# A linear-attention block and a gated FFN on one core: queues in a new written order, one PSUM ring, 64-row products together, matmuls on zeros

## The chip, the cores and the metric

The kernel runs on one core of a Trainium2 chip. A core has four engines with instruction queues of their own that work in order: TensorE (PE in the profile; its weight loads are the row PEld), VectorE (DVE), ScalarE (ACT) and GpSimd (POOL). SyncE (SP) only issues DMAs; GpSimd issues DMAs too, and its queue (q0) can cast float32 to float16 on the way. The metric is the device time of one execution in microseconds (us), lower is better.

## What is computed

```python
# q, k, v: (8 batches, 8 heads, 576 positions, 64)
q_s = softmax(q, axis=-1)                     # over the 64 features
k_s = softmax(k, axis=2)                      # over the 576 positions
kv  = einsum('bhsd,bhse->bhde', k_s, v)       # a 64x64 matrix for each head
x   = einsum('bhsd,bhde->bhse', q_s, kv)      # -> (4608 tokens, 512)
a, b = x @ w1, x @ w2                         # (4608, 1024) each
out = ((a * b) @ w3) @ w_out                  # (4608, 512)
```

All inputs and the output are float32; the matrix products run in float16 with float32 accumulation.

## The kernel before

**Folding.** `w3 @ w_out` is worked out once, in eight row blocks `ft`: `w3t` (line 441) transposes a block of w3 on TensorE, `w3T` copies it out of PSUM, `pf` (line 451, eight matmuls of 512 columns a block) multiplies it with w_out, and `W3O` scales it out of PSUM. `pf.ft.0` needs the first half of w_out (`wo.0`), `pf.ft.1` the second.

**Attention, for each batch b.** On k: `kmx` (maximum over positions), `cb` (the same across partitions, a chain of small VectorE steps), `ksub`, `kexp`. On q, in two parts p (four and five of nine position groups; 1024 and 1280 elements a partition): `qmx`, `qsub`, `qexp`, `qsm` (sum), `qeps`, `qrc` (reciprocal), `qn`. The normalized q is transposed on TensorE for batches 0 and 1 (`qt`, line 642, then the copy `qT`) and by a DMA on SP for the others (`qd`). `kv` (lines 562 and 571) multiplies k and v, `kv2` divides, and the product with q comes in three pieces: `xm.b.0` and `xm.b.1` (four matmuls of 64 rows and 512 columns each, line 668) and the rest `xt.b` (eight of 64 columns, the same line). `xs` and `xts` scale them out of PSUM into x. v is cast by the load in batches 0 and 1 and by `vc` in the others.

**FFN, for each chunk c** (one for each batch, and a ninth of the positions that `xt` left over). For each of eight blocks u, `up.1` (x @ w2, line 793), its copy `bs` out of PSUM, `up.0` (x @ w1, the same line), and `ab` (line 808), the product of both on VectorE; each `up` is four matmuls of 128 rows and 512 columns. Chunk 1 is worked in two halves. Then four `down` (line 815; 830 in the ninth chunk), eight matmuls each, whose results `os` copies out of PSUM and `st` stores from SP.

**PSUM.** It has eight banks. Before, they are three pools: four banks for `pab` (up, w3t), two for `po` (down, pf) and two for `att` (kv, qt, xm, xt). A product `xm` or `xt` takes two banks, so the next one waits until `xs` has emptied both.

**The order.** `Plan` holds the steps with their needs. `Plan.order` walks through time with a length in us for each step, `LEADS` (an offset for each kind of step) and `PICKS` (which engine takes a step that has a choice), and emits the steps in the order that it finds; `LOADS` gives the order of the first loads. Within 50 us of that walk, `link` makes a step of VectorE or GpSimd that uses their shared port wait for the last one of the other engine. Loads of q, k and v of batch 0 and 1 and of the weights go out on GpSimd (only `q.0.0` on SP), those of later batches on SP in the order k, q, v. SP's first load of batch 2 waits until `w1.2`, the last load on GpSimd but one, has landed. On GpSimd a load waits until the eighth before it has landed.

Of the kernel before, what the change touches and what calls it, by code (L numbers as in the profile page):

```python
# [13 lines left out]
ALU = mybir.AluOpType  # L14
# [3 lines left out]
class Plan:  # L18


    RATE = 409.0e3
    LAND = 1.7
    HOP = 0.15
    NEAR = 0.2
    LINKED = 50.0
    BUS = 2.2
    BEGIN = {"SP": 0.74, "POOL": 1.25, "DVE": 1.0, "ACT": 1.0, "PE": 1.0}

    def __init__(self, rings, leads, picks):
        self.rings = rings  # L30
        self.leads = leads
        self.picks = picks
        self.steps = {}

    @staticmethod
    def key(name):


        if name[0] == "up":
            return f"up{name[1]}_{min(name[2], 3)}"  # L40
        if len(name) > 2 and name[1] < 2 and name[0] not in ("bs", "ab", "down", "os", "st", "pf"):
# [892 lines left out]
```

## Time and profile before

| | |
|---|---|
| three runs | 245.95, 247.72 and 247.88 us (median 247.72) |
| the profiled execution | 244.56 us, of which the span from first to last instruction is 242.7 us |
| TensorE busy | 227.2 us (94%), 1884 matmuls |
| VectorE busy | 180.3 us (74%) |
| ScalarE, GpSimd busy | 120.4 us (50%), 118.2 us (49%) |
| first matmul, end of the last | 9.9 us, 239.4 us |
| read from memory, written | 38.80 MB, 9.44 MB |

Busy time is counted per engine, so overlapping work counts on each. TensorE's matmuls are pipelined, and a busy TensorE is not one at its peak. The chain of waits follows back from the last instruction what released it, and so names the work that set the end; an engine off that chain costs nothing by being idle.

### The profile page before, as it was taken

How to read it: one execution, taken by the hardware profiler on the slowest of the kernel's cores; microseconds unless marked ns; L12 is line 12 of the kernel's file. 1: busy time of each engine (PE TensorE's matmuls, PEld its weight loads, DVE VectorE, ACT ScalarE, POOL GpSimd, SP SyncE). 2: the span in 40 equal slices, each digit the busy share in tenths (PEclk: the TensorE clock that was granted, in tenths of full speed). 3: DMA queues.
4: the chain of work that ended last, by engine and by line, in shares of the span. 5: the costliest groups of instructions: out<-in, count | busy, mean ns of one | idle time of the engine just before them, and what ended most of it. 6: DMA issues, size and time to landing. Idle time of an engine off the chain costs nothing.

```text
span 242.7 us, 4757 instructions
## 1 busy us (share of the span) xinstructions
PE 227.2 (94%) x1884; PEld 112.1 (46%) x1884; DVE 180.3 (74%) x306; ACT 120.4 (50%) x183; POOL 118.2 (49%) x79
## 2 busy tenths in 40 slices
PE   0398899999999999999999999999999999999994
PEld 0245644454886444344444444444444344444443
DVE  2889869969998989989998999799876154335320
ACT  2367767536867657545543664466433522121112
POOL 8446276508996788279445946595462000000000
PEclk9999999999999999999999999999999999999999
DMA  6999999999998994993999089801940230022153
GB/s 229 234 265 251 260 298 196 248 398 391 354 151 292 388 171 123 399 219 67 324 384 177 0 309 375 173 4 36 131 108 3 58 72 0 3 64 66 43 130 130
DMA packets 37766, 45.65 MB, mean 188 GB/s; under 512 B 15985, under 2 KB 21873, under 8 KB 37745
## 3 DMA queue, kind: packets, MB, share of 16 engines
q1 hardware_dynamic: 30080, 34.74, 50.9%
q0 software_dynamic: 7664, 10.62, 20.4%
q8 instruction: 14, 0.23, 0.4%
q14 instruction: 8, 0.06, 0.1%
HBM read 38.80 MB, written 9.44 MB: 199 GB/s over the span
## 4 chain that ended last, share of the span: by engine, by line
PE 90%; DMA 6%; POOL 2%; issue 1%; ACT 1%; ACTq 0%; POOLq 0%
PE pab L793 52%; PE po L815 23%; DMA w<-in_moe_w_dram 6%; PE po L451 4%; PE po L830 3%; PE pkv L562 2%; PE xm L668 2%; PE w3t L441 1%; PE xt L668 1%; PE qtp L642 1%; POOL w L403 1%; PE pkv L571 1%; ACT w3T L342 0%; POOL wosb L403 0%; POOL k L403 0%
## 5 line engine op out<-in xcount | busy, mean ns | idle before, releaser
L808 DVE TENSOR_TENSOR ab<-pab,bsb 128x512 f16<-128x512 f32 x72 | 49.0, 687 | 24.8 <-PE pab L793 19.3
L793 PE MATMUL pab<-x,w2sb 128*128 128x512 f16 (+1 forms) x288 | 65.9, 356 | 0.0
L793 PE MATMUL pab<-x,w1sb 128*128 128x512 f16 (+1 forms) x288 | 65.9, 356 | 0.0
L815 PE MATMUL po<-W3O,ab 128*128 128x512 f16 x256 | 59.3, 380 | 0.0
L342 ACT CAST bsb<-pab 128x512 f16<-128x512 f32 x49 | 28.5, 582 | 40.6 <-PE pab L793 40.5
L793 PEld LDWEIGHTS <-w1sb 128*128 128x128 f16 x320 | 30.7, 98 | 30.0
L793 PEld LDWEIGHTS <-w2sb 128*128 128x128 f16 x320 | 30.5, 98 | 29.3 <-issue 0.2
L537 POOL TENSOR_TENSOR k<-k,cb 128x1152 f32<-128x1152 f32 x14 | 36.5, 2623 | 10.5 <-issue 7.9
L627 POOL TENSOR_TENSOR en<-eq,qr 128x1024 f16<-128x1024 f16 (+1 forms) x14 | 29.3, 2096 | 21.9 <-issue 9.1
L815 PEld LDWEIGHTS <-ab 128*128 128x128 f16 x256 | 23.8, 98 | 29.7 <-issue 2.9
L595 POOL TENSOR_TENSOR q<-q,qm 128x1280 f32<-128x1280 f32 (+1 forms) x13 | 27.7, 2145 | 13.7 <-DVE rc L580 11.7
L342 ACT COPY osb<-po 128x512 f32<-128x512 f32 (+1 forms) x28 | 15.9, 569 | 35.8 <-PE po L815 31.0
L479 DVE TENSOR_REDUCE km<-k 128x128 f32<-128x1152 f32 x12 | 25.8, 2149 | 0.0
L590 DVE TENSOR_REDUCE qm<-q 128x16 f32<-128x1024 f32 (+1 forms) x16 | 21.5, 1345 | 5.7 <-DMA q<-in_q_dram 5.7
L603 ACT ACTIVATE eq<-q 128x1024 f16<-128x1024 f32 (+1 forms) x16 | 18.6, 1164 | 13.7 <-POOL q L595 6.9
L545 ACT ACTIVATE ek<-k 128x1152 f16<-128x1152 f32 x16 | 18.6, 1163 | 6.5 <-POOL k L537 5.1
L608 DVE TENSOR_REDUCE qr<-eq 128x16 f32<-128x1024 f16 (+1 forms) x16 | 21.2, 1324 | 0.1
L342 DVE CAST bsb<-pab 128x512 f16<-128x512 f32 x23 | 15.8, 685 | 5.2 <-PE pab L793 4.0
L451 PE MATMUL po<-wosb,w3T 128*128 128x512 f16 x64 | 16.8, 408 | 1.2 <-issue 0.6
L346 ACT ACTIVATE x<-xm 128x512 f16<-128x512 f32 x30 | 16.5, 598 | 1.7 <-PE xm L668 1.7
L441 PE MATMUL w3t<-ident,w 128*128 128x128 f16 x64 | 5.8, 249 | 11.0 <-DMA w<-in_moe_w_dram 11.0
L342 ACT COPY w3T<-w3t 128x1024 f16<-128x1024 f16 x8 | 8.0, 1016 | 6.4 <-PE w3t L441 5.9
(60 smaller groups left out, 172.0 us busy)
## 6 DMA issues: line engine op xcount, KB each, us to landing
out_dram<-osb SPq DMA_DIRECT2D x66, 128.0 KB, 2.4
k<-in_k_dram SPq DMA_DIRECT2D x6, 1152.0 KB, 5.8
q<-in_q_dram SPq DMA_DIRECT2D x6, 1152.0 KB, 9.3
v<-in_v_dram SPq DMA_DIRECT2D x6, 1152.0 KB, 11.9
k<-in_k_dram POOLq DMA_DIRECT2D x2, 1152.0 KB, 10.8
q<-in_q_dram POOLq DMA_DIRECT2D x2, 640.0 KB, 14.7
v<-in_v_dram POOLq DMA_DIRECT2D x2, 576.0 KB, 12.9
w<-in_moe_w_dram POOLq DMA_DIRECT2D x2, 512.0 KB, 10.9
```

The costliest lines, as they stand in the source:

```text
L342: return [(nc.scalar.copy if eng == "ACT" else engine[eng].tensor_copy)(out=out, in_=in_)]
L451: nc.tensor.matmul(st["pf", ft], lhsT=st["w3T", ft][:, gt, :], rhs=wosb[:, gt, :], start=(gt == 0), stop=(gt == N_FT - 1))
L479: dve.tensor_reduce(out=st["km", b][:, two(hp), :], in_=kb[:, two(hp), :, :].rearrange("p h j d -> p h d j"), axis=AX.X, op=ALU.max)
L537: return [engine[eng].tensor_tensor(out=kb[:, two(hp), :, :], in0=kb[:, two(hp), :, :], in1=st["cb", b][:, two(hp), None, :].broadcast_to( ...
L545: nc.scalar.activation(out=st["ek", b][:, hp, :, :].rearrange("p j (i d) -> p i j d", i=2), in_=kb[:, two(hp), :, :], func=AF.Exp)
L590: dve.tensor_reduce(out=st["qm", b][:, :, j], in_=qb[:, :, j, :], axis=AX.X, op=ALU.max)
L595: return [engine[eng].tensor_tensor(out=qb[:, :, j, :], in0=qb[:, :, j, :], in1=st["qm", b][:, :, j, None].broadcast_to([P, HH, n, D]), op ...
L608: dve.tensor_reduce(out=st["qr", b][:, :, slice(*PARTS[p])], in_=st["eq", b, p], axis=AX.X, op=ALU.add)
L627: return [engine[eng].tensor_tensor(out=st["en", b][:, j, :, :].rearrange("p j h d -> p h j d"), in0=st["eq", b, p], in1=st["qr", b][:, :, ...
L793: nc.tensor.matmul(st["p", one, c, sub, u][:, a * (t1 - t0):(a + 1) * (t1 - t0)], lhsT=w[:, ct, fb * P:(fb + 1) * P], rhs=x()[:, ct, t0:t1 ...
L808: dve.tensor_tensor(out=st["ab", c][:, nf * u:nf * u + nf, t0:t1], in0=cut(st["p", 0, c, sub, u]), in1=cut(st["bsb", c, sub, u]), op=ALU.mult)
L815: nc.tensor.matmul(st["po", c, tb], lhsT=st["ab", c][:, ft, tb * P:(tb + 1) * P], rhs=W3O[:, ft, :], start=(ft == 0), stop=(ft == N_FT - 1))
```

## The change

- **The order is written out.** `Plan.order`, `LEADS`, `PICKS` and `LOADS` are gone. `ORDER` names each step once, with `/A`, `/D` or `/P` for ScalarE, VectorE or GpSimd where there is a choice, and `Plan.run` emits them in that order; each engine's queue is the part of it that the engine has. `late` and `kind` only describe steps. `link` is made along the whole order, up to the last step of VectorE that uses the port.
- **Loads.** On GpSimd the order is q.0.1, k.0, w3.4, w3.2, wo.0, wo.1, w3.1, q.1.1, w3.0, v.0, w3.3, k.1, w2.0, w1.0, w2.1, w1.1, q.1.0, w2.2, w1.2, w2.3, w1.3, v.1, w3.5. Before it was k.0, w3.4, wo.0, w3.2, wo.1, q.0.1, w3.0, q.1.0, w3.3, v.0, w3.5, q.1.1, w3.1, w2.0, k.1, w1.0, w2.3, w2.1, w1.1, w2.2, w1.3, w1.2, v.1. So w3.5 (blocks 6 and 7 of the fold) moves from the eleventh place to the last, and these two blocks are folded at the start of chunk 1. SP's first load of batch 2 is now q.2, and waits (`GATE = 3`) until w1.3, the third from the end, has landed; q.2, q.3, v.2, k.2 follow in this order.
- **Engines.** VectorE gets four `w3T`, one `W3O`, `ksub.1.0`, `ksub.1.1`, `qsub.1.1`, `qn.1.0` and four more `xs` than before, and gives up `qsub.0.1` (now on GpSimd), both `qT` and three `xts`; in the later batches some `bs`, `os` and `qn` change places too.
- **PSUM** is one ring of eight banks for everything: a new tile takes the bank of the tile eight before it and waits until that is free.
- **The 64-row products** xm.b.0, xm.b.1 and xt.b stand next to each other in TensorE's queue in all batches but batch 1, where xm.1.0 and xm.1.1 are neighbours and xt.1 follows kv.2. Before, four to eight `pf`, `up` or `down` matmuls or more stood between them.
- **43 matmuls on zeros** of 512 columns: 13 and 20 ahead of the first transposes of w3, 10 between the third of these and `pf.2.0`. VectorE sets the zeros beforehand.
- The second identity matrix, which nothing used, is gone.

```diff
+    def text(name):
+        return ".".join(str(x) for x in name)
+
+    def run(self, order, link):
+        byname = {self.text(n): s for n, s in self.steps.items()}
+        listed = [t.partition("/")[::2] for t in order.split()]
+        assert sorted(t for t, _ in listed) == sorted(byname), set(byname) ^ {t for t, _ in listed}
+        twos = [i for i, (t, c) in enumerate(listed) if byname[t]["port"] and self.CODES.get(c, "DVE") == "DVE"]
         held = None
+        for i, (t, code) in enumerate(listed):
+            s = byname[t]
+            eng = s["eng"]
+            if isinstance(eng, tuple):
+                eng = self.CODES[code]
+                assert eng in s["eng"], t
+                got = s["emit"](eng)
+            else:
+                got = s["emit"]()
+            if s["port"] and eng != "ACT" and held and i <= twos[-1] and held[0] != eng:
+                link(got[0], held[1])
+            if s["port"] and eng != "ACT":
+                held = eng, got[-1]
+
+
+EARLY = [("q", 0, 0)]
+GATE = 3
...
+ORDER = """
+zero.0 q.0.0 qmx.0.0 qsub.0.0/D zero.1 q.0.1 qmx.0.1 qexp.0.0 qsm.0.0 k.0 kmx.0.0 cb.0 w3.4 ident w3t.5 w3.2
+w3t.2 w3t.4 zero.2 w3T.5/D wo.0 w3T.2/A pf.2.0 pf.5.0 wo.1 pf.5.1 pf.2.1 w3.1 q.1.1 w3.0 v.0 w3.3 qsub.0.1/P
+qexp.0.1 qeps.0.0/D ksub.0.1/D kexp.0.1 w3T.4/A k.1 qrc.0.0 qn.0.0/P qt.0.0 qT.0.0/A w2.0 w3t.1 pf.4.0 pf.4.1
+qsm.0.1 qeps.0.1/D qrc.0.1 ksub.0.0/D w1.0 qn.0.1/P w3T.1/D W3O.2/A W3O.4/A kexp.0.0 W3O.5/A qmx.1.1
+qsub.1.1/D qexp.1.1 w3t.0 w3T.0/D pf.1.0 qt.0.8 qT.0.8/A pf.1.1 W3O.1/D kv.0 qt.0.16 qsm.1.1 qeps.1.1/A w3t.3
+qT.0.16/A w3T.3/A pf.0.0 pf.0.1 W3O.0/A qrc.1.1 kv2.0 xm.0.0 xs.0.0.0/A xm.0.1 xs.0.1.0/A xt.0 xts.0.1/A
+xs.0.0.1/A xs.0.1.1/A pf.3.0 qn.1.1/D pf.3.1 W3O.3/A kmx.1.0 cb.1 qt.1.8 qT.1.8/A xts.0.0/A qt.1.16 up.1.0.0.0
+bs.0.0.0/A up.0.0.0.0 up.1.0.0.1 up.0.0.0.1 bs.0.0.1/A ksub.1.1/D w2.1 w1.1 up.1.0.0.2 up.0.0.0.2 up.1.0.0.3
+bs.0.0.2/A qT.1.16/A bs.0.0.3/A q.1.0 qmx.1.0 ab.0.0.0 qsub.1.0/D qexp.1.0 ab.0.0.1 ab.0.0.2 w2.2 up.0.0.0.3
+up.1.0.0.4 qsm.1.0 ksub.1.0/D ab.0.0.3 bs.0.0.4/A w1.2 up.0.0.0.4 kexp.1.1 kexp.1.0 qeps.1.0/D ab.0.0.4
+qrc.1.0 qn.1.0/D up.1.0.0.5 bs.0.0.5/A up.0.0.0.5 ab.0.0.5 w2.3 up.1.0.0.6 w1.3 up.0.0.0.6 bs.0.0.6/A ab.0.0.6
+up.1.0.0.7 bs.0.0.7/A v.1 kv.1 kv2.1 qt.1.0 up.0.0.0.7 w3.5 w3t.7 w3T.7/D ab.0.0.7 q.2 qmx.2.1 qsub.2.1/P
+qmx.2.0 qsub.2.0/P w3t.6 qT.1.0/A xm.1.0 xm.1.1 pf.7.0 w3T.6/A pf.6.0 pf.7.1 xs.1.0.1/A xs.1.1.1/A xs.1.0.0/A
+up.1.1.0.0 bs.1.0.0/D pf.6.1 up.0.1.0.0 q.3 qmx.3.1 qsub.3.1/P ab.1.0.0 qmx.3.0 qsub.3.0/P qexp.2.1 xs.1.1.0/A
+W3O.6/A up.1.1.0.1 bs.1.0.1/A W3O.7/A up.0.1.0.1 up.1.1.0.2 up.0.1.0.2 down.0.0 up.1.1.0.3 bs.1.0.2/A qsm.2.1
+qeps.2.1/D up.0.1.0.3 up.1.1.1.0 up.0.1.1.0 qrc.2.1 ab.1.0.1 qexp.2.0 qsm.2.0 ab.1.0.2 qexp.3.1 down.0.1
+down.0.2 down.0.3 qn.2.1/P bs.1.0.3/A qexp.3.0 os.0.1/A bs.1.1.0/A os.0.2/A os.0.0/A qeps.2.0/D v.2 vc.2.1/P
+k.2 kmx.2.0 kmx.2.1 qrc.2.0 up.1.1.1.1 up.0.1.1.1 bs.1.1.1/A os.0.3/A vc.2.0/P cb.2 ab.1.0.3 qsm.3.0 ab.1.1.0
+qsm.3.1 up.1.1.1.2 q.4 v.3 qmx.4.1 q.5 qmx.5.1 ab.1.1.1 st.0.1 st.0.2 k.3 qn.2.0/P ksub.2.1/P qd.2.1 qd.2.0
+st.0.0 down.1.0 kexp.2.1 bs.1.1.2/A qeps.3.1/A up.0.1.1.2 up.1.1.1.3 bs.1.1.3/D ksub.2.0/P kexp.2.0 kv.2 k.4
+kv2.2 os.1.0/A st.1.0 st.0.3 xt.1 xts.1.1/A ab.1.1.2 up.0.1.1.3 ab.1.1.3 qrc.3.1 qeps.3.0/A xts.1.0/A down.1.1
+os.1.1/A st.1.1 v.4 qmx.4.0 xm.2.1 xm.2.0 xs.2.0.0/D xs.2.0.1/A xt.2 down.1.2 xs.2.1.1/A xs.2.1.0/A up.1.2.0.0
+up.0.2.0.0 up.1.2.0.1 up.0.2.0.1 os.1.2/A st.1.2 bs.2.0.0/A qsub.4.1/P qexp.4.1 xts.2.1/A xts.2.0/A vc.3.0/P
+qrc.3.0 qn.3.0/P qsub.5.1/P qsub.4.0/P qexp.4.0 q.6 qn.3.1/P kmx.3.0 kmx.3.1 ab.2.0.0 qmx.5.0 cb.3 ksub.3.1/P
+down.1.3 os.1.3/A qd.3.1 qd.3.0 st.1.3 up.1.2.0.2 up.0.2.0.2 bs.2.0.1/A bs.2.0.2/A vc.4.1/A qexp.5.1
+up.1.2.0.3 up.0.2.0.3 up.1.2.0.4 bs.2.0.4/A vc.3.1/A up.0.2.0.4 kmx.4.0 ab.2.0.1 ab.2.0.2 up.1.2.0.5
+up.0.2.0.5 up.1.2.0.6 bs.2.0.3/D ab.2.0.3 bs.2.0.5/A ab.2.0.4 ab.2.0.5 bs.2.0.6/D up.0.2.0.6 up.1.2.0.7
+up.0.2.0.7 ab.2.0.6 kexp.3.1 ksub.3.0/P kexp.3.0 kv.3 bs.2.0.7/D ab.2.0.7 down.2.0 os.2.0/A qsub.5.0/P
...
+up.1.8.0.6 up.0.8.0.6 st.7.3 st.7.2 bs.8.0.5/A bs.8.0.6/A ab.8.0.6 ab.8.0.5 up.1.8.0.7 bs.8.0.7/D up.0.8.0.7
+ab.8.0.7 down.8.0 os.8.0/A down.8.1 os.8.1/A down.8.2 os.8.2/D st.8.0 st.8.1 st.8.2 down.8.3.0 os.8.3.0/D
+st.8.3.0 down.8.3 os.8.3/A st.8.3
+"""
...
-    pab_pool = ctx.enter_context(tc.tile_pool(name="pab", bufs=4, space=bass.MemoryType.PSUM))
-    po_pool = ctx.enter_context(tc.tile_pool(name="po", bufs=2, space=bass.MemoryType.PSUM))
-    att_pool = ctx.enter_context(tc.tile_pool(name="att", bufs=2, space=bass.MemoryType.PSUM))
-    plan = Plan({"pab": 4, "po": 2, "att": 2, "osb": 4, "eq": 4, "bsb": 4, "w3T": 2}, LEADS, PICKS)
-
+    banks = ctx.enter_context(tc.tile_pool(name="banks", bufs=8, space=bass.MemoryType.PSUM))
+    plan = Plan({"ps": 8, "osb": 4, "eq": 4, "bsb": 4, "w3T": 2})
+
+    def bank(shape, dtype, name):
+        return banks.tile(shape, dtype, tag="ps", name=name)
...
-    WARM = 0
+    ZEROS = [13, 20, 10]
...
+    zero = konst.tile([P, 512], F16)
+    dve.memset(zero, 0.0)
+
+    def zeros(i, n):
+        def go():
+            st["zero", i] = bank([P, 512], F32, "zero")
+            for _ in range(n):
+                nc.tensor.matmul(st["zero", i], lhsT=zero[:, 0:P], rhs=zero, start=True, stop=True)
+
+        plan.add(("zero", i), "PE", go, takes="ps", gives=[("zero", i)], size=n)
+
+    for i, n in enumerate(ZEROS):
+        zeros(i, n)
...
+    gates = {}
+
+    def load(name, queue):
         dst, src, last = side(name)
 
         def go():
             st[name] = (nc.sync if queue == "SP" else g_).dma_start(out=dst, in_=src)
+            gate = gates.get(name)
             if gate:
                 tc.add_manual_dep(
                     st[name].ins, st[gate].ins.name,
                     mybir.DependencyInfo(mybir.DependencyClass.Sync, mybir.DependencyReason.DATA),
                     reason="load order")
 
...
+    names = [("w3", i) for i in range(len(ROWS))] + [("wo", i) for i in range(len(FOLD))]
+    names += [(n, i) for n in ("w1", "w2") for i in range(len(COLS))]
+    names += [n for b in range(2) for n in (("k", b), ("q", b, 0), ("q", b, 1), ("v", b))]
+    for name in names:
+        load(name, "SP" if name in EARLY else "POOL")
+    for b in range(2, B):
+        for n in "kqv":
+            load((n, b), "SP")
+    if len(listed) > 1:
+        loads = [n for n in listed if plan.steps.get(n, {}).get("kind") == "load"]
+        gates[[n for n in loads if plan.steps[n]["eng"] == "SP" and n not in EARLY][0]] = [
+            n for n in loads if plan.steps[n]["eng"] == "POOL"][-GATE]
+    plan.add(("ident",), "POOL", lambda: make_identity(nc, ident16))
...
-                st[(*name, i)] = p_att([P, len(hp_list), (j1 - j0) * HALF], F32, name[0])
+                st[(*name, i)] = bank([P, len(hp_list), (j1 - j0) * HALF], F32, name[0])
...
-                st["p", one, c, sub, u] = p_ab()
+                st["p", one, c, sub, u] = bank([P, 512], F32, "pab")
...
-            xn = XS[c][sub] if c < B else [("xts", b, i) for b in range(B) for i in range(2)]
-            A(("up", 1, c, sub, u), "PE", 0.87, up(sub, u, 1), xn + prev + ws("w2", u), takes="pab")
+            A(("up", 1, c, sub, u), "PE", up(sub, u, 1), xn[0] + prev + ws("w2", u), takes="ps",
+              kind="up" + half, late=[(n, 2) for n in xn[-1]] if len(xn) > 1 else [])
```

## The prediction

> **What bounds the kernel now.** I read the page first (the span, busy shares and chain of waits), then the chain in order of time, then busy time by window, then the first 30 us as a timeline, last the landing time of each early load.
>
> The page:
>
> ```profile
> span 242.7 us, 4757 instructions
> ...
> PE 227.2 (94%) x1884; PEld 112.1 (46%) x1884; DVE 180.3 (74%) x306; ACT 120.4 (50%) x183; POOL 118.2 (49%) x79
> ...
> PE 90%; DMA 6%; POOL 2%; issue 1%; ACT 1%; ACTq 0%; POOLq 0%
> ```
>
> TensorE is on the chain for 90% of the span. So the time is the start, TensorE's own work, and a tail. Busy time in some windows (columns: PE, PEld, DVE, ACT, POOL, clock, DMA, GB/s):
>
> ```profile
> 0.00:6.00 6.00, 0.00 (x0) 0.00 (x0) 1.64 (x6) 1.49 (x2) 4.95 (x12) 1.00 0.66 228
> 6.00:12.00 6.00, 1.93 (x16) 1.68 (x16) 5.23 (x11) 2.02 (x3) 2.90 (x7) 1.00 1.09 238
> 12.00:18.00 6.00, 5.59 (x24) 2.47 (x24) 5.06 (x9) 4.07 (x5) 2.72 (x4) 1.00 1.07 265
> 18.00:24.00 6.00, 4.98 (x41) 3.13 (x42) 5.89 (x5) 4.88 (x7) 4.21 (x5) 1.00 1.15 251
> 24.00:30.00 6.00, 5.38 (x144) 3.67 (x143) 5.07 (x11) 4.31 (x7) 1.48 (x2) 1.00 1.13 259
> ...
> 60.00:90.00 30.00, 30.00 (x295) 19.40 (x294) 27.12 (x50) 20.72 (x35) 25.16 (x15) 1.00 1.01 278
> ```
>
> From 36 us on TensorE never rests: 30.00 of 30. What it loses lies ahead: 9.9 us until w3.4 has landed, and some 2.2 us in gaps up to 36 us. There the DMAs are full (share above 1), so the early part is set by the order of arrival. VectorE is the next engine, with 27.12 of 30. The start as a timeline shows the other loss:
>
> ```profile
> 9.92 1.93 PE L441 MATMUL w3t<-ident,w 128*128 128x128 f16 x16 [9.92 <-DMA w<-in_moe_w_dram]
> ...
> 12.39 3.36 PE L451 MATMUL po<-wosb,w3T 128*128 128x512 f16 x8 [0.55 <-DMA wosb<-in_moe_w_out_dram]
> ...
> 16.10 1.89 PE L451 MATMUL po<-wosb,w3T 128*128 128x512 f16 x8
> ```
>
> The same eight matmuls take 3.36 us at 12.4 us and 1.89 at 16.1: TensorE runs at about half speed for its first 5.5 us. Last the chain in one batch (start, us, what):
>
> ```profile
> 88.53 6.91 PE pab L793 x32
> ...
> 98.87 0.34 PE xm L668 x4
> 99.21 1.83 PE po L815 x8
> 101.04 0.34 PE xm L668 x4
> 101.38 1.83 PE po L815 x8
> 103.21 0.18 PE xt L668 x8
> 103.40 7.01 PE pab L793 x32
> 110.41 1.73 PE po L815 x8
> ```
>
> Eight `down` matmuls take 1.73 us, but 1.83 right after a 64-row product; 32 `up` 6.91, but 7.01. So each change from 64 rows back costs 0.10.
>
> **Part 1, products together.** Four products at 0.216 (1.73/8) run side by side in four quarters, so 0.34 is 0.21 of work and 0.13 of fixed cost. In batch 1 the eight of 256 columns take 0.34 too, two rounds of 0.107 and again 0.13 once: the second round costs only its work. A batch pays now 0.34+0.10+0.34+0.10+0.18+0.10 = 1.16. Together it is 0.34 + 0.21 + 0.05 (xt, two rounds of 64 columns) + 0.10 = 0.70, so 0.45 saved. It counts seven times after the first `up` (batch 1, where xt.1 joins kv.2 instead, about the same): **3.15 us**. Bounds: 0, if the second product always waits for banks, and 3.2. I take 3.15; batch 1 is the nearest row.
>
> **Part 2, the start.** The bytes are the same, so the last GpSimd load again lands at about 47 us (47.4 now). In the new order, at the spacings of the landings now (w3.4 2.33, half of w_out 2.5, a 256 KB weight part 1.1 to 1.4, v 2.8, k.1 2.9, q.0.1 1.82, q.1.1 3.04): q.0.1 6.0, k.0 9.4, w3.4 11.8, w3.2 12.9, wo.0 15.4, wo.1 17.9, w3.1 19.0, q.1.1 21.4, w3.0 22.5, v.0 25.3, w3.3 26.4, k.1 29.3, w2.0 30.6, w1.0 31.8, w1.3 41.5, v.1 44.4, w3.5 47.0. q.0.1 goes past k.0 and w3.4 and costs them 1.8 each; w3.4 was at 9.9. GpSimd issues each load in 0.54 to 0.94 us, with at most eight outstanding, and is never late for one.
>
> Thirteen zero matmuls at 0.42 and twenty at 0.216 are 5.5 + 4.3 us, from 1.7 (VectorE has set the zeros; a 128x36 memset took 0.09 us, a 128x1024 copy 0.68, and it is idle until 4.6) to 11.5. That is inside the wait for w3.4: no cost, and the clock is up by then. With that cover gone they would cost 9.8. The ten later ones (2.2) stand between w3t.4, done at 13.9, and pf.2.0, whose data (wo.0, and w3T.5 on VectorE after cb.0) are there at 15.7: 0.4 late at most.
>
> Then: pf.5 waits for wo.1 (17.9), pf.4 ends at 22.6, w3t.0 with w3.0 at 23.1, pf.1 at 25.2, kv.0 at 26.8. VectorE: qmx.1.1 22.9, qsub.1.1 24.8, w3T.0 and W3O.1 26.2, qsm.1.1 27.7, ScalarE's qeps and qrc 28.3, kv2.0 29.3. The products of batch 0 go at 29.3, pf.3 ends at 31.8, the last transposes at 32.3; ScalarE has the five copies of x done by 32.7, the first ones earlier. First `up` at **32.5** instead of 37.0. Bounds 31 (q.1.1 at 1.82) and 34 (q.1.1 at 3.04 and the chain after it).
>
> But two fold blocks are still to do: 2 x (0.49 + 1.73) = **4.4** back. So the earlier start is nearly all borrowed. Two more transposes and xt.0 are done ahead: 0.4.
>
> **Part 3, VectorE.** Its net gain of work by the rows: four w3T (0.68) 2.7, a W3O 0.7, four xs 2.75, two ksub (1.36) 2.7, a qsub 1.5, two qn 2.5, two os 1.2, qeps 0.4, less two bs, three xts and the qT, 3.2: 11 us, about 9 of it before 60 us. By the windows it has worked 47.6 us of the first 60 now, and can begin at 4.6: so 56 to 57 us of work for 55. Laid out row by row, its queue is never idle from 16 us to some 94 us. TensorE then waits in four places: xm.1.0 for kv2.1 (0.6), kv.2 for the chain cb.2, ksub.2.1, ksub.2.0, kexp.2.0 (0.5), xt.1 for its bank, which ab.1.1.1 gives back after qmx.4.1 and qmx.5.1 (0.65), and up.1.2.0.5 for the bank of ab.2.0.1, behind kmx.3 and cb.3 (1.1). That is 2.85. The other end is 0: in 60 to 90 us now VectorE is 90% busy and TensorE waits for nothing. I take the middle, **1.4**: a VectorE at 100% on paper lies between that row and the full layout, which lets each wait fall on TensorE undiminished. Queued behind a waiting `ab` are the next qmx and kmx, which the batch two ahead needs much later.
>
> **Part 4, what costs nothing.** SP's loads q.2, q.3, v.2, k.2 go out from 41.5 on and land 2.9 us apart, k.2 at about 56; kmx.2 comes at 63. The port links along the whole order make GpSimd wait for VectorE; GpSimd is busy for 118 of 243 us. If it were late, ksub.4 and qn.4 would be first: qn.4.1 and its DMA transpose (4.3 to landing) end within 1 us of xm.4. The second identity (0.5 on GpSimd) was hidden.
>
> **The sum.** TensorE now goes from 37.0 to 239.4: 202.4. Plus 4.4, less 0.4, less 3.15: 203.3. The tail of 3.3 after the last matmul stays. 32.5 + 203.3 + 1.4 + 3.3 = **240.5 us of span against 242.7**, 2.2 less (0.9%). The profiled execution itself took 244.56; the median of the runs is 247.72, 5.0 above the span. I add the same 5.0: **245.5**. A measurement here can tell about 1% (2.5 us) from no change.
>
> **Rivals.**
>
> *TensorE never waits, and the start is earlier (0.17).* For it: 30.00 of 30 now. Against: VectorE's 9 us more. Without the 1.4, and with the first `up` 0.6 earlier: 238.5, so 243.5.
>
> *The last loads come late (0.12).* When w1.3 has landed, SP starts four loads of 1152 KB while v.1 and w3.5 are still on GpSimd's queue. If both queues share the engines evenly, v.1 and w3.5 take 10.8 instead of 5.4 us, w3.5 lands at 52.3, and w3t.7, due at about 49.5, waits 2.8; some 0.6 of it replaces xm.1's wait: 242.7, so 247.7. Against: v.1 now landed 2.86 after w1.2, as v.0 did alone (2.81), though SP's k.2 was out. The Trainium skill, DMA: Bandwidth & Descriptors, section Queues, rings and completion order, says that an engine takes turns between the queues that have work, a packet at a time. By that rule this rival is the case; the trace does not agree so far, with 2.86 against 2.81.
>
> *The products don't merge (0.09).* Three of them need six of eight banks; if each waits for its banks, the 3.15 is gone: 243.7, so 248.7.
>
> *Slower: VectorE becomes the bound (0.15).* From 18 to 42 us VectorE was idle for 3.8 of 24 us, waiting for loads and for GpSimd's use of the port. If it loses these 3.8 again, now that it has no slack, everything behind it in its queue moves by that, and TensorE with it: 32.5 + 203.3 + 2.85 + 3.8 + 3.3 = 245.7, so 250.7. It decides the sign once VectorE loses more than 0.7 us beyond the full layout (242.0). For it: it is one queue in order, and the first `up` hangs on kv2.0. Against: its waits for data fall while TensorE has folds to do.
>
> **How the numbers follow.** The forecast has 0.47 (its own range 244 to 247.2). Just under half of it, and the first rival, lie more than 1% below: 0.40. Slower by over 1% is the last rival and a tail of the fourth: 0.17. The rest, 0.43, is within 1%. The range goes from 241 (no waits, first `up` at 31, a run at the low end of the 1.8 us that the runs differ by) to 251 (VectorE as the bound).
>
> **What would show it.** Right: matmuls on zeros from about 2 us, 0.42 then 0.216 each; w3t at about 12; first `up` at 32 to 33; two xm and xt in one piece of some 0.6; TensorE idle 1 to 2 us between 45 and 95, put down to VectorE. Wrong: TensorE without a gap after 33 us; xm pieces still apart; w3t.7 waiting for w3.5; VectorE idle between 18 and 42.

## The result, and the profile after

The kernel after the change takes **249.17 us** (median of 20 runs), the kernel before 246.60 (20 runs beside them): ratio **1.0115, interval 1.0086 to 1.0144**. It became slower by about 1%, where 245.5 us, 0.9% less than before, had been forecast. The profiled execution took 248.26 us with a span of 246.5. The page of the kernel after:

```profile
span 246.5 us, 4820 instructions
...
PE 233.9 (95%) x1927; PEld 117.3 (48%) x1927; DVE 196.2 (80%) x318; ACT 112.3 (46%) x177; POOL 107.2 (43%) x72
...
PE 64%; DMA 17%; DVE 11%; POOL 3%; issue 2%; ACT 2%; DVEq 0%; POOLq 0%; ACTq 0%
```

TensorE is still busy for nearly all of the time, but it makes up only 64% of the chain that ended last, where it was 90%. DMA, VectorE and GpSimd now stand in the chain, so TensorE waits for them somewhere in the middle. VectorE is busy for 15.9 us more than before; the prediction had counted 11. (Busy time of VectorE also holds time in which an instruction stands and waits, as will be seen.)

The start, as a timeline of TensorE (start, us, instruction, the idle time before it and what ended it), is what was forecast:

```profile
1.55 9.71 PE L240 MATMUL zero<-zero 128*128 128x512 f16 x33 [1.55 <-DVE zero L234]
12.07 0.71 PE L315 MATMUL w3t<-ident,w 128*128 128x128 f16 x8 [0.81 <-DMA w<-in_moe_w_dram]
...
16.54 3.62 PE L325 MATMUL pf<-wosb,w3T 128*128 128x512 f16 x16
```

The zeros fill the wait for w3.4, and the first sixteen fold matmuls take 3.62 us, full speed. The first `up` starts at 32.6 us. The products of a batch together are there too, in the chain of waits in order of time:

```profile
149.71 0.56 PE xm L518 x8
150.27 0.06 PE xt L518 x8
150.33 3.56 PE po L650 x16
```

With the 0.10 that the sixteen `down` take over 3.46 (16 at 0.216), that is 0.72 us a batch instead of 1.16. From the first `up` on there should then have been 203.3 us of work and 1.4 of waits. The last matmul ends at 243.15, so 210.55 us have gone by, 7.25 more than the work. By the windows TensorE was busy for 204.40 of them and **idle for 6.15**. The same timeline of TensorE shows where:

```profile
70.38 1.03 PE L628 MATMUL pab<-x,w1sb 128*128 128x256 f16 x8 [0.39 <-DVE ab L643]
76.29 0.80 PE L412 MATMUL pkv<-v,ek 64*64 64x65 f16 x72 [0.53 <-ACT ek L395]
82.14 0.63 PE L518 MATMUL xm<-qT,kv 64*64 64x512 f16 x8 [2.27 <-DMA qT<-en]
...
120.70 0.77 PE L412 MATMUL pkv<-v,ek 64*64 64x65 f16 x72 [0.66 <-DVE ab L643]
125.26 0.82 PE L518 MATMUL xm<-qT,kv 64*64 64x512 f16 x8 [1.09 <-DVE kv L433]
...
193.18 0.39 PE L650 MATMUL po<-W3O,ab 128*128 128x512 f16 x1 [0.20 <-DVE ab L643]
194.57 2.12 PE L650 MATMUL po<-W3O,ab 128*128 128x512 f16 x9 [1.00 <-DVE ab L643]
```

These are xm.2 (2.27, for the DMA transposes of batch 2), batch 4 (0.66 at kv.4, 1.09 at xm.4, and 0.33 within xt.4: 2.1 together), and down.6.0 (1.00, with 0.20 just before it); 0.53 had been foreseen, and 0.39 lies near a wait that had been. That is 6.5 us of waits with the 0.33, which counts as busy. The last 0.8 of the 7.25 is busy time that the sum of the work did not have. Busy time by window (PE, PEld, DVE, ACT, POOL, clock, DMA, GB/s) says the same of the stages:

```profile
60.00:90.00 30.00, 26.82 (x253) 16.23 (x251) 27.64 (x42) 14.42 (x27) 21.59 (x13) 1.00 1.03 299
90.00:120.00 30.00, 30.00 (x220) 13.54 (x217) 28.55 (x48) 18.91 (x30) 22.48 (x11) 1.00 1.06 282
120.00:150.00 30.00, 28.25 (x285) 13.12 (x288) 28.64 (x48) 15.93 (x24) 15.51 (x9) 1.00 0.59 153
```

In 60 to 90 TensorE loses 3.2 of 30 us, in 120 to 150 it loses 1.75, and between them nothing, though VectorE is as busy there. So a full VectorE alone is not the answer; each place needs its own cause.

One more thing has to be known to read the times: in 9 of the 20 executions after, the mean granted clock is about 0.992 (one at 0.984) and the time some 1.9 us longer (median 250.28 against 248.42 for the other eleven). That is the half-clock window dealt with below. Where "at full clock" is written, these executions are left out, and spans are given as medians of the others; that of the kernel after is 246.6 us. The kernel before, run again beside each group of experiments, had median spans from 243.2 to 244.8 us, so a difference of about 1 us between two groups says little by itself.

### The profile page after: what moved, and what is told of

Read it like the earlier page. It is cut to its first block, busy times and chain, and to the rows that moved or that the text cites. A ratio compares the mean times of both kernels' runs of the same rounds, so it can differ in the third digit from the quotient of the medians.

```text
span 246.5 us, 4820 instructions
## 1 busy us (share of the span) xinstructions
PE 233.9 (95%) x1927; PEld 117.3 (48%) x1927; DVE 196.2 (80%) x318; ACT 112.3 (46%) x177; POOL 107.2 (43%) x72
## 4 chain that ended last, share of the span: by engine, by line
PE 64%; DMA 17%; DVE 11%; POOL 3%; issue 2%; ACT 2%; DVEq 0%; POOLq 0%; ACTq 0%
PE pab L628 37%; PE po L650 16%; DMA v<-in_v_dram 6%; DMA q<-in_q_dram 4%; DVE ab L643 4%; DMA qT<-en 3%; DMA k<-in_k_dram 3%; PE pf L325 3%; PE po L665 3%; DVE km L356 3%; PE pkv L412 2%; DVE en L477 2%; PE xm L518 2%; POOL k L387 2%; DVE qr L466 1%
## 5 line engine op out<-in xcount | busy, mean ns | idle before, releaser
L643 DVE TENSOR_TENSOR ab<-pab,bsb 128x512 f16<-128x512 f32 x72 | 47.4, 681 | 16.6 <-PE pab L628 9.1
L387 POOL TENSOR_TENSOR k<-k,cb 128x1152 f32<-128x1152 f32 x12 | 31.3, 2626 | 33.6 <-DVE cb L383 26.1
L445 POOL TENSOR_TENSOR q<-q,qm 128x1280 f32<-128x1280 f32 (+1 forms) x12 | 25.4, 2125 | 22.1 <-DVE qm L440 17.2
L477 POOL TENSOR_TENSOR en<-eq,qr 128x1024 f16<-128x1024 f16 (+1 forms) x12 | 25.5, 2125 | 13.3 <-DVE qr L470 13.0
L214 ACT COPY osb<-po 128x512 f32<-128x512 f32 (+1 forms) x26 | 14.9, 581 | 35.6 <-PE po L650 24.7
L453 ACT ACTIVATE eq<-q 128x1024 f16<-128x1024 f32 (+1 forms) x16 | 18.5, 1165 | 15.9 <-POOL q L445 10.1
L214 DVE CAST bsb<-pab 128x512 f16<-128x512 f32 x21 | 14.4, 684 | 2.9 <-PE pab L628 2.4
L218 ACT ACTIVATE x<-xm 128x512 f16<-128x512 f32 x26 | 14.3, 605 | 4.6 <-PE xm L518 2.3
L325 PE MATMUL pf<-wosb,w3T 128*128 128x512 f16 x64 | 15.1, 379 | 0.0
L214 DVE COPY osb<-po 128x512 f32<-128x512 f32 (+1 forms) x11 | 7.2, 660 | 9.6 <-PE po L650 5.2
L240 PE MATMUL zero<-zero 128*128 128x512 f16 x43 | 12.0, 447 | 1.6 <-DVE zero L234 1.6
```

The source lines that it names most:

```text
L214: return [(nc.scalar.copy if eng == "ACT" else engine[eng].tensor_copy)(out=out, in_=in_)]
L325: nc.tensor.matmul(st["pf", ft], lhsT=st["w3T", ft][:, gt, :], rhs=wosb[:, gt, :], start=(gt == 0), stop=(gt == N_FT - 1))
L387: return [engine[eng].tensor_tensor(out=kb[:, two(hp), :, :], in0=kb[:, two(hp), :, :], in1=st["cb", b][:, two(hp), None, :].broadcast_to( ...
L445: return [engine[eng].tensor_tensor(out=qb[:, :, j, :], in0=qb[:, :, j, :], in1=st["qm", b][:, :, j, None].broadcast_to([P, HH, n, D]), op ...
L453: nc.scalar.activation(out=st["eq", b, p], in_=qb[:, :, j, :], func=AF.Exp)
L477: return [engine[eng].tensor_tensor(out=st["en", b][:, j, :, :].rearrange("p j h d -> p h j d"), in0=st["eq", b, p], in1=st["qr", b][:, :, ...
```

## The experiments

Tokens with `/P`, `/A`, `/D` are steps put on GpSimd, ScalarE, VectorE. All edits are to the kernel after; the diffs show only the tokens that matter.

### The three places one by one

**The transposes of batch 2 before k.3** (e1).

```diff
- st.0.2 k.3 qn.2.0/P ksub.2.1/P qd.2.1 qd.2.0 st.0.0 down.1.0
+ st.0.2 qn.2.0/P ksub.2.1/P qd.2.1 qd.2.0 st.0.0 k.3 down.1.0
```

> Only the place of one load on SP changes: k.3 goes out behind the two DMA transposes of batch 2 and the store after them, not ahead of them. Theory A (the transposes wait behind loads): the transpose of part 0 lands before 80 us instead of 82.0, the 2.27 us that xm.2 waited for it go, and the span falls from 246.5 to about 244.3. Theory B (VectorE's one queue is the bound, and each wait of TensorE is a symptom of it): the wait comes back at the next place where TensorE needs VectorE, in batches 3 and 4, and the span stays above 246.

Measured: 246.45 us, ratio to before 1.0007 (0.9971 to 1.0044), span at full clock 244.2. The wait at xm.2 is gone and the other waits of over 0.5 us are as they were. SP's issues and the landing of the two transposes, first in the kernel after the change, then in this one:

```profile
69.28 0.57 SPq L287 DMA_DIRECT2D k<-in_k_dram  x1
69.94 8.46 SPq L500 DMA_TRANSPOSE qT<-en  x2
...
DMA to landing us min/median/max: 8.3/9.0/9.6
```

```profile
69.44 4.20 SPq L499 DMA_TRANSPOSE qT<-en  x2
...
75.02 1.65 SPq L286 DMA_DIRECT2D k<-in_k_dram  x2
...
DMA to landing us min/median/max: 4.2/4.8/5.4
...
79.83 0.63 PE L517 MATMUL xm<-qT,kv 64*64 64x512 f16 x8
```

The transposes now land 4.2 and 5.4 us after their issue, instead of 8.3 and 9.6. One load of 1152 KB, issued 0.7 us ahead of them, was worth 2.4 us.

**kmx.5.0 later** (e2). VectorE's k maximum of batch 5 (2.15 us) stands between kv.4 and kv2.4.

```diff
- qeps.5.0/D kmx.5.0 kexp.4.0 kv.4 kv2.4 bs.3.0.6/A ab.3.0.6 v.6
+ qeps.5.0/D kexp.4.0 kv.4 kv2.4 bs.3.0.6/A ab.3.0.6 kmx.5.0 v.6
```

> Only one step on VectorE changes its place: kmx.5.0 (2.15 us) goes behind kv2.4 and ab.3.0.6. Theory A (single misplaced steps): xm.4 no longer waits 1.09 us for kv2.4, and its tail piece not the 0.33 after it: span 245.1. Theory B (VectorE's queue is the bound): the 2.15 us come out a little later, since kmx.5.0 is still to be done before cb.5, and the span stays within 0.4 of 246.5.

Measured: 248.92 us, ratio 1.0100 (1.0028 to 1.0173). The span is 246.1 at full clock, in two executions. The wait at xm.4 went, and down.3.0 waited 1.41 us for ab.3.0.7, now behind kmx.5.0: theory B. Here a wait only moved; VectorE was late at this place, and the order of two steps did not mend it.

**The last qn on GpSimd** (e3).

```diff
- qn.7.1/D ... qn.7.0/D
+ qn.7.1/P ... qn.7.0/P
```

> qn.7.1 and qn.7.0 go from VectorE to GpSimd, as the kernel before had them. Theory A: on VectorE qn.7.1 took 3.12 us beside GpSimd's ksub.7.1 where it takes 1.49 alone; without it the copies bs.6 and products ab.6 come earlier, and down.6.0 waits 1.2 us less: span 245.3. Theory C (it is not the port but the amount of work on VectorE there): the same gain, but GpSimd's steps keep their usual 2.62 and 1.15 us either way, so vc.7.0 would still take 2.41 as it does now; under A it goes back to 1.15.

Measured: 246.89 us, ratio 1.0035 (0.9995 to 1.0075), at full clock 244.95: 1.7 less. The waits at down.6.0 are gone. What had been slow in the kernel after can be read in its timeline of VectorE and GpSimd:

```profile
181.06 5.20 POOL L387 TENSOR_TENSOR k<-k,cb 128x1152 f32<-128x1152 f32 x2 [18.36 <-DVE cb L383]
...
184.48 3.12 DVE L477 TENSOR_TENSOR en<-eq,qr 128x1280 f16<-128x1280 f16 x1
186.19 2.41 POOL L214 CAST v<-v 128x1152 f16<-128x1152 f32 x1
```

qn.7.1 took 3.12 us on VectorE beside GpSimd's ksub.7.1, and 1.48 where nothing ran beside it; GpSimd's cast took 2.41 and, with qn gone from VectorE, 1.16. This is theory A. qn.7.1 ended 1.3 us after ksub.7.1, and the cast 1.0 us after qn.7.1, as if each had stood until the one before it was done. ksub.7.1 comes behind the last step that the port links cover.

**All three edits at once** (e4).

> The three edits together. Theory A, with each place on its own: 2.3 + 1.4 + 1.2 less, span about 241.6, a little below the kernel before (242.7), ratio to it about 0.995. Theory B: the sum is not reached, 244 or more, ratio 1.005 or more.

Measured: 245.29 us, ratio 0.9978 (0.9947 to 1.0008), at full clock 243.35 instead of the 241.6 of the sum. The 1.41 at down.3.0 is most of what is missing: the second edit had not removed a cause.

### The other parts of the change

**No zeros** (e5; `ZEROS = []`, their tokens left out).

> The changed kernel without its 43 matmuls on zeros (the part of the change that warms the clock is undone), nothing else changed. Theory D (the zeros bring the clock up for the first folds, though in about half of the runs a window of 3.4 us at half clock comes back): without them every run starts at half speed for some 5.5 us after 12 us, and the runs lie together at about the slow half of the changed kernel, span 248 to 248.5. Rival: the first folds wait for data and for VectorE anyway, and the span is 246.5 as with zeros.

Measured: 249.08 us, ratio 1.0112 (1.0051 to 1.0173): about the same as with them. The span is 247.3 at full clock, between the two theories, and none of the four executions has the half-clock window. The first `up` starts at 34.29 us in the timeline, against 32.44 with zeros; but the wait at xm.2 is 0.16 instead of 2.27, since the transposes land at 81.5 us here and at 82.0 there. Most of what the zeros win at the start was handed to the next late transfer.

**More zeros** (e6; `ZEROS = [13, 34, 10]`), until w3.4 has landed.

> The changed kernel with 34 zero matmuls in the second group instead of 20 (3.0 us more, to about 13.4 us), so that TensorE does not idle before w3.4 lands. Theory D: no run has the half-clock window, all runs lie with the full-clock runs of the changed kernel, span 246 to 247, median of the runs 248.3 instead of 249.2. Rival (the window comes at random, whatever TensorE does in those 3 us): about half of the runs still show a clock of 0.993 and spans near 248.5. Cost under both: none, since pf.2.0 cannot start before 15.5.

Measured: 248.95 us, ratio 1.0118 (1.0059 to 1.0177). In the profile w3t starts at 14.16 right behind the zeros, the first `up` at 33.9, and xm.2 waits 2.04: no gain either. Two of the six executions still have a mean clock of 0.991, against theory D.

**Products of batches 5 and 6 apart** (e7), as before the change.

```diff
- xm.5.0 xm.5.1 xt.5 ... down.4.1 ... down.4.2
+ xm.5.0 down.4.1 xm.5.1 down.4.2 xt.5
- xm.6.0 ... xm.6.1 ... xt.6 ... down.5.2 down.5.3
+ xm.6.0 down.5.2 ... xm.6.1 ... down.5.3 xt.6
```

> The changed kernel with the 64-row products of batches 5 and 6 taken apart again: one down between the two xm, one between the second xm and xt. Prediction of the change's own term (0.45 a batch for keeping them together): span 0.9 more than the changed kernel, about 247.4 at full clock, the chain showing 0.34, 1.83, 0.34, 1.83, 0.18 in those two batches. Rival: later waits (down.6.0 for ab.6.7) swallow it, and the span stays at 246.5.

Measured: 254.23 us, ratio 1.0314 (1.0242 to 1.0385), 251.6 of span at full clock: 5 us more, where 0.9 was the price of the products. The timeline shows why:

```profile
156.04 0.29 DVE L219 TENSOR_SCALAR xtail<-xt 128x128 f16<-128x128 f32 x1 [3.96 <-PE xt L517]
156.24 2.12 DVE L355 TENSOR_REDUCE km<-k 128x128 f32<-128x1152 f32 x1
158.29 0.67 DVE L219 TENSOR_SCALAR x<-xm 128x512 f16<-128x512 f32 x1
159.01 0.38 PE L627 MATMUL pab<-x,w2sb 128*128 128x512 f16 x1 [2.07 <-DVE x L219]
```

VectorE's queue has the eviction of xt ahead of kmx.6.0 and of the last x. With xt 4.35 us behind the first xm instead of 0.45, it stood idle for 3.96 us and then came late with x. The products together are worth keeping, and more than their own time depends on them in a queue written for them. What they are worth by themselves this run does not show.

### Moving VectorE's steps

**Four edits** (f1): those of e1 and e3, kmx.5.0 behind xs.4.0.0, qmx.7.1 behind cb.5, and the longer zeros.

> The edits of e1 (k.3 behind the transposes) and e3 (qn.7 on GpSimd), 34 zeros in the second group, and on VectorE kmx.5.0 behind xs.4.0.0 and qmx.7.1 behind cb.5. Theory A with D: 2.3 and 1.4 less as measured, the two waits of batch 4 (0.66 and 1.1 to 1.4) gone, no half-clock runs: span 241 to 242, ratio to the kernel before 0.988. Theory B (VectorE's queue is the bound): the waits of batch 4 come back in the next batch and the span is 243 or more, ratio 0.995.

Measured: 247.93 us, ratio 1.0064 (1.0025 to 1.0103). The waits up to 130 us are gone but for 0.52 at kv.2, and kv.5 waits instead (0.53 and 1.83, for ksub.5.1 on GpSimd, which stands behind VectorE's later steps). The span is 244.2 at full clock: theory B.

**Six edits** (f2 and f3): those of e1 and e3, kmx.5.0 behind xs.4.0.0, qmx.7.1 behind kmx.6.1, os.3.0 to os.3.2 on ScalarE, ksub.5.1 ahead of qn.5.0; with the first zeros and with the longer ones. The diff has part of them.

```diff
- ksub.5.0/P down.3.0 down.3.1 os.3.0/D os.3.1/D qmx.6.1
+ kmx.5.0 ... ksub.5.0/P down.3.0 down.3.1 os.3.0/A os.3.1/A qmx.6.1
- qn.5.0/P ... ksub.5.1/P
+ ksub.5.1/P qn.5.0/P
```

> The transposes of batch 2 ahead of k.3 and the last qn on GpSimd, as before, and four steps of VectorE's row around batch 4 moved: kmx.5.0 behind xs.4.0.0, qmx.7.1 behind kmx.6.1, the evictions os.3.0 to os.3.2 from VectorE to ScalarE, and ksub.5.1 ahead of qn.5.0 on GpSimd. Theory A (the waits are an order of VectorE's steps that can be mended, since ScalarE stands idle for 7 us just there): the 1.41 us at down.3.0 of the three edits together and the 2.6 us at kv.5 of the four edits both go, only the 0.53 us at kv.2 is left, a span of 241.8 to 242.5 us at the full clock and 244.2 us by the median, ratio 0.993. Theory B (VectorE has no room between 60 and 150 us, so a wait taken away at one batch comes back at the next): 1.5 us or more come back at kv.5, down.4.0 or xm.5, and the time stays at 245.3 us or above.

> The same with 14 more zeros ahead of w3.4, so that TensorE is busy until w3.4 is there (13.2 us). Theory C (the half clock comes from the idle 2 to 3 us before w3.4): no run with a clock of 0.993, all spans within 0.7 us, some 0.3 to 0.8 us above the full-clock runs of the kernel with fewer zeros, as first pf starts later by what the zeros overhang. Theory D (it comes from something else, since 8 of 12 runs of the four edits with this many zeros had a clock of 0.992 and were 2 us longer): about half of the runs have it again, and a profile that falls into one shows the half clock at another place than behind the wait for w3.4.

Measured: 243.62 us, ratio 0.9923 (0.9890 to 0.9957), and 244.05 us, 0.9921 (0.9887 to 0.9956). The first lies a little below the 244.2 of theory A. Both beat the kernel before by 0.8%, so VectorE's work fits. This goes round the cause in batch 4; it does not name it.

### Why a transpose is late beside a load

**Batch 2's transposes on ScalarE's DMA queue** (e8), k.3 left where it is.

```diff
- nc.sync.dma_start_transpose(out=
+ (nc.scalar if b == 2 else nc.sync).dma_start_transpose(out=
```

> The kernel after the change, with the two transposes of batch 2 issued by ScalarE's DMA queue instead of SP's; k.3 and the loads ahead of it stay where they are. Theory A (transposes wait behind the loads that the same queue issued before them): they land 4 to 5 us after their issue, though k.3 is still under way, and the 2.27 us at xm.2 shrink to what ScalarE's own delay gives (its exponentials for kv.2 stand behind the two issues, some 2 to 4 us). Theory B (they share the 16 DMA engines with k.3, whichever queue issues them): they still take 8 us or more.

```profile
69.54 0.51 SPq L286 DMA_DIRECT2D k<-in_k_dram  x1
...
70.35 1.45 ACTq L499 DMA_TRANSPOSE qT<-en  x1
71.89 6.80 ACTq L499 DMA_TRANSPOSE qT<-en  x1
...
DMA to landing us min/median/max: 9.5/9.9/10.2
```

The lines are k.3's issue and the two on ScalarE's queue (start, us), 0.8 us and more behind it. The transposes took 9.5 and 10.2 us to land, as theory B has it: a queue of their own did not free them from the load. Issuing the second one also held ScalarE for 6.80 us, so kv.2 waited 5.92 us (252.44 us in the one run, which has the half-clock window too). The Trainium skill, DMA: Bandwidth & Descriptors, section Queues, rings and completion order, says that each DMA engine takes turns between the queues it has work for. This run is in line with that, with 9.5 to 10.2 us on a queue of their own against 8.3 to 9.6 behind the load. It is no proof that they share the engines: how long transposes from ScalarE's queue take with no load beside them was not run. What did help was to move the load (4.2 and 5.4 in the first experiment).

### Why VectorE is late in batch 4

VectorE's additions `qeps` (a constant added to 128x20 or 128x16 numbers) took 1.3 us for seven before the change, 188 ns each. After it nine take 8.6 us, 956 ns each (the columns are busy us, mean ns and idle time ahead):

```profile
L616 DVE TENSOR_SCALAR qr<-qr 128x20 f32<-128x20 f32 (+1 forms) x7 | 1.3, 188 | 0.2
```

```profile
L466 DVE TENSOR_SCALAR qr<-qr 128x20 f32<-128x20 f32 (+1 forms) x9 | 8.6, 956 | 0.1
```

VectorE and GpSimd in the kernel after:

```profile
107.83 5.19 POOL L387 TENSOR_TENSOR k<-k,cb 128x1152 f32<-128x1152 f32 x2 [7.52 <-ACT xtail L218]
108.71 1.76 DVE L466 TENSOR_SCALAR qr<-qr 128x20 f32<-128x20 f32 x1
112.98 4.21 POOL L477 TENSOR_TENSOR en<-eq,qr 128x1024 f16<-128x1024 f16 x2
113.59 1.33 DVE L466 TENSOR_SCALAR qr<-qr 128x20 f32<-128x20 f32 x1
...
120.10 2.34 POOL L477 TENSOR_TENSOR en<-eq,qr 128x1280 f16<-128x1280 f16 x1
121.67 0.81 DVE L466 TENSOR_SCALAR qr<-qr 128x16 f32<-128x16 f32 x1
```

Each of the three ends within 0.05 us of the GpSimd instruction beside it: at 110.47, 114.92 and 122.48, where the first of the two ksub ends at 110.45, the first of the two en at 114.89 and the last en at 122.44. The Trainium skill, SBUF — State Buffer, section SBUF: two separate sides, calls the port pair that VectorE and GpSimd share an exclusive lock, which a GpSimd instruction, or a VectorE one in a two-port mode, holds until its end. These rows agree, with 0.18 us alone and up to 1.76 beside GpSimd; that `qeps` runs in such a mode no view shows. `qeps` has no `port=True` in the plan, so no link keeps it clear. To test whether this is the cause or only fills time, the tokens, which stand apart in the order, were run by themselves (e9), with e1's edit (f4) and with the six edits (f5):

```diff
- qeps.2.1/D qeps.2.0/D qeps.4.1/D qeps.5.1/D qeps.5.0/D qeps.7.1/D
+ qeps.2.1/A qeps.2.0/A qeps.4.1/A qeps.5.1/A qeps.5.0/A qeps.7.1/A
```

> The kernel after the change, with the six steps qeps.2.1, 2.0, 4.1, 5.1, 5.0 and 7.1 (an addition of a constant to 128x20 or 128x16 numbers) moved from VectorE to ScalarE at the same places of the order. In the trace after, these six took 1.63, 0.36, 1.76, 1.33, 0.81 and 1.67 us, where the same step took 0.18 before, and most of them end when the GpSimd instruction then running ends. Theory A (VectorE is late because these small steps stand until GpSimd gives the shared port free): VectorE's busy time falls by 6 to 7 us, the waits at kv.4 (0.65), xm.4 (1.09) and in xt.4 (0.33) go and that at down.6.0 (1.2) mostly, the wait at xm.2 for the transposes stays at 2.0 to 2.8 us, a span of 242.9 to 244.5 us at the full clock. Theory B (VectorE's row is full with its own work, and the time of these steps is taken out of waits that it would have anyway; or ScalarE's row in order now waits in their place): VectorE's waits grow by what it saves, and the span stays above 245.5 us at the full clock.

> The same, and k.3 behind the transposes of batch 2 on SP. Theory A: two causes that add, the wait at xm.2 goes too, a span of 240.4 to 242.2 us at the full clock, the median of the times at 243 us (0.988 of before). Theory B: no better than the transposes alone, 244.1 us of span.

> The order that has been the best so far (kmx.5.0 behind xs.4.0.0, qmx.7.1 behind kmx.6.1, three evictions on ScalarE, qn.7 on GpSimd, k.3 behind the transposes), and the six qeps on ScalarE. Its full-clock spans were 241.2 to 241.6 us with waits of 0.5 at kv.2 and 0.6 at kv.5 left. Theory A: VectorE has 6 us to spare that it does not need there; at most these two waits go, 240.5 to 241.4 us. Theory B: ScalarE, which has taken three evictions already, is late at kv.5 or for a bank: 242 us or more.

Measured: 247.35 us (1.0044, 1.0006 to 1.0081), 247.12 (1.0028, 0.9993 to 1.0064) and 245.75 (0.9974, 0.9934 to 1.0013), with spans of 245.15, 244.1 and 243.0 at full clock. A miss in the totals, and yet telling. In the first VectorE's busy time fell by 5.8 us and all three waits of batch 4 went, as theory A had it. But down.6.0 kept its waits in the two kernels that leave qn.7 on VectorE, so they are qn's own, and a wait of 2.4 us at kv.2 was new in all three:

```profile
70.63 0.32 ACT L463 ACTIVATE qr<-qr,epst 128x16 f32<-128x16 f32 x1
...
71.31 1.91 POOL L476 TENSOR_TENSOR en<-eq,qr 128x1024 f16<-128x1024 f16 x1 [4.50 <-DVE qr L469]
...
79.89 0.80 PE L411 MATMUL pkv<-v,ek 64*64 64x65 f16 x72 [2.44 <-ACT ek L394]
```

On ScalarE qeps.2.0 stands behind evictions that wait for TensorE, so qn.2.0, ksub.2 and kexp.2 behind it are late: theory B, but at batch 2 alone.

### The three causes together, no order changed

k.3 behind the transposes, qn.7 on GpSimd, and of the qeps only 4.1, 5.1 and 5.0 on ScalarE (e10); then the same with the longer zeros (f6).

```diff
- qeps.4.1/D qeps.5.1/D qeps.5.0/D qn.7.1/D qn.7.0/D
+ qeps.4.1/A qeps.5.1/A qeps.5.0/A qn.7.1/P qn.7.0/P
```

> The kernel after the change with three small edits and no other step moved: k.3 behind the transposes of batch 2 on SP; qeps.4.1, qeps.5.1 and qeps.5.0 on ScalarE (those of batch 2 stay on VectorE, since on ScalarE they made kv.2 wait 2.44 us); qn.7.1 and qn.7.0 on GpSimd. Theory A (three causes, each one taken away without moving the wait elsewhere): the waits of 2.27 at xm.2, 2.07 around kv.4 and xm.4 and 1.20 at down.6.0 all go, 0.4 and 0.5 at ab.1.0.3 and kv.2 stay, so 246.3 - 5.5 = 240.8 us of span at the full clock (240.3 to 241.4), about what the prediction's sum said (240.5 with 1.4 us of waits). The longer runs with a clock of 0.993 or less are left in some of the executions, since the wait for w3.4 is left. Theory B (VectorE as the bound: what is taken away at one batch comes back at the next): 242.5 us or more at the full clock, with a wait of over 1 us at a place where there was none.

> The same with 14 more zeros, up to where w3.4 lands. Theory C (TensorE falls to half clock for 3.4 us where it has waited some 2 us or more, at whatever place): no wait of over 1 us is left behind the first zeros, so no execution with a clock of 0.993 or less, where the kernel without the added zeros has some; full-clock spans 0.3 to 0.8 us longer. Theory D (the lower clock has to do with the chip or with the zeros themselves): as many such executions as without the added zeros.

Measured: **243.00 us, ratio 0.9904 (0.9866 to 0.9942)**, and 243.28 us, 0.9902 (0.9864 to 0.9940). The span at full clock is 240.8 us, the number expected. Page and windows of the first:

```profile
PE 233.5 (97%) x1927; PEld 117.5 (49%) x1927; DVE 188.3 (78%) x313; ACT 113.2 (47%) x180; POOL 110.2 (46%) x74
...
60.00:90.00 30.00, 29.32 (x265) 17.29 (x263) 28.71 (x47) 16.75 (x30) 23.74 (x13) 1.00 1.00 318
...
120.00:150.00 30.00, 30.00 (x235) 13.70 (x233) 28.16 (x49) 17.79 (x28) 15.33 (x8) 1.00 0.58 143
```

VectorE is as full as in the kernel after the change in these stages (28.2 to 28.7 of 30), and TensorE waits for 1.0 us in all from the first `up` on. So VectorE's load was not the bound; three causes were. Two of them had been taken away alone: 2.4 us for the transposes and 1.65 for qn.7 leave 242.55, and the three qeps, which no run moved by themselves, bring 1.75 more, beside 2.1 us of waits. With six steps moved (k.3, two qn, three qeps) the changed kernel is 1% faster than the one before.

### The half clock

The low window could be seen where a profile had one. In the kernel of six edits it lies behind the wait for w3.4, in the one with six edits and `qeps` behind the 2.44 us at kv.2 (windows of the two, the first row from the former):

```profile
15.00:18.00 3.00, 3.00 (x10) 1.09 (x9) 3.00 (x6) 2.62 (x3) 1.92 (x3) 0.50 1.04 206
```

```profile
78.00:81.00 3.00, 2.83 (x88) 2.31 (x89) 2.80 (x9) 1.23 (x5) 2.30 (x2) 0.52 0.89 259
```

It lasts 3.41 us by the clock's records. Among 12 runs of the six edits two had it, and none of the 10 with zeros up to w3.4; of the three causes 3 of 12, and with the longer zeros none of 9. In these two longer-zero kernels no wait of over 0.6 us is left. The longer zeros did not help where a wait was left: 8 of 12 in f1, with 1.83 us at kv.5, and 2 of 6 in e6, with 2.04 at xm.2. This speaks for theory C, a long wait at any place; the numbers are small, no profile of f1 or e6 shows the window, and where the limit lies was not measured. Behind 1.14 us at w3.4 one execution had it, behind 1.29 another did not; one with the products apart had it behind 1.00 at down.6.0, while the 2.27 at xm.2 in the kernel after was not followed by it. In the clock's records the full-speed stretches before and after such windows are whole multiples of 3.41 us (6.83, 10.24, 51.20, 71.68 and 75.09 among them), so whether a wait brings the window may hang on how it lies on this grid; that was not tested.

## Why the prediction was wrong

**Part 3 and Part 4, the waits after the first `up`: the steps that failed.** The sum took 1.4 us for them, bounds 0 and 2.85; the listed ones are 6.5. VectorE, with the exponentials that wait for it, makes 4.2 of these, and the transposes of batch 2 make 2.27. The kinds of mistake differ by place.

- *Part 3's term for qeps was mis-sized*: 0.4 for two more steps, 7.3 in fact, because it priced them with the row of before (0.18), where GpSimd was not running beside them. That made batch 4 wait 2.1 us. The list of four foreseen waits stopped at 94 us, since VectorE's layout fell behind only until there.
- *Part 3's qn at the end*: two more qn were taken at 2.5 us and cost 4.1; the one beside ksub.7.1 took twice its time, and down.6.0 waited 1.2 us. The fourth part even named the port links, but as a wait of GpSimd, and not what happens past their end.
- *Part 4, "what costs nothing"*: it followed SP's loads of batch 2 and asked whether they land in time, and looked at the transposes of batch 4. The transposes of batch 2 beside k.3 were put at nothing, with the 4.3 us to landing taken for granted. They took 8.3 and 9.6, and xm.2 waited 2.27 us.
- Foreseen and found: kv.2 (0.5, measured 0.53). At xt.1 a wait of 0.65 for a bank was foreseen; there is none, but one of 0.39 at an `up` some 6 us earlier (70.4 us). The waits at xm.1.0 and up.1.2.0.5 are not there.

**Part 2, the start,** was right in its times (w3t at 12.07 for 11.8, first `up` at 32.6 for 32.5), and in its statement that nearly all is borrowed. "The clock is up by then" held in 11 of the 20 executions; in the other nine it fell back, and they took some 2 us longer.

**Part 1** was right: 0.72 us a batch, for 0.70.

**The work term** was 0.5 short: with the three causes gone, first `up` at 32.65 and last matmul at 237.51 leave 204.9 us, 1.0 of waits and 203.8 of busy TensorE, for 203.3 by the sum. The span of 240.8 is close to the forecast's 240.5, in part by luck: the start was 0.15 later, the work 0.5 longer and the waits 0.4 shorter than in the sum. So the sum fits the kernel without its three faults.

**The offset.** Each execution takes 1.8 us more than its span. The 5.0 added was the gap between one profiled execution and a median; that execution lay at the low end of the kernel before, whose median span is 243.2 to 244.8 us beside the experiments. With 1.8 the forecast would have been 242.3, so by luck this hid 3.2 us of the error. 240.5, 5.9 more from the first `up` to the last matmul, 0.1 at the start and 1.8 give 248.3, the profiled time; the executions with the half clock lift the median from 248.42 to 249.17.

**The rivals.** The rival of the last loads did not come true: w3t.7 (48.4 us) did not wait. Its thought, that transfers out at the same time delay each other, fits xm.2, though there the load and the transposes were on one queue. The slower rival named VectorE as the bound, with 3.8 us of waits for loads and for GpSimd's port from 18 to 42 us. Port and sign were right, stretch and form not: VectorE was idle for only 1.65 us there, and `qeps` stood beside GpSimd at 59, 109 to 122 and 182 us.

## What to carry to other kernels

When steps change engine, price them with what runs beside them in the new place, tiny ones too: a 0.18 us addition became 1.76. When a transfer moves, ask which small transfers on the critical path are in flight with it, perhaps on another queue too. And before calling an engine the bound, give each of its waits a cause and take that cause away alone; a wait that only moves (e2) and one that goes (e10) look alike in the busy shares.

## What the hardware showed

- A wait of TensorE of 1.0 to 3.0 us was followed in some executions by 3.41 us at half clock, and such executions took some 2 us longer (a later landing of w3.4, which goes with the longer waits there, may be a part of that). The Trainium skill, TensorE: Matmul & The Clock Gate, Part 1, puts the fall after about one idle window of 3.4 us. Here shorter waits were enough (2.36 us in the kernel of six edits), and the length of the low stretch agrees.
- A 128x20 addition on VectorE, 0.18 us alone, took up to 1.76 us and ended with the GpSimd instruction beside it.
- A DMA transpose took twice its time (8.3 to 9.6 for 4.2 to 5.4 us) beside one load of 1152 KB; on ScalarE's queue it took 9.5 to 10.2 beside the load.
